# Turning the keys of the late units on VectorE and in SBUF transfers, instead of on TensorE

## The chip, the cores and the metric

The kernel runs on one core of a Trainium2 chip. The metric is the device time of one execution in microseconds; before the change it is 658.83 us, the median of three runs (657.85 to 659.45). The profiled execution has a span of 656.8 us.

## What is computed

The program is a gated linear attention followed by an MLP. All data are float32.

```
f = sigmoid(f_logit)                         # (4, 8, 768, 48): batch, heads, tokens, D
for t in range(768):
    state = f[t][:, None] * state + outer(k[t], v[t])   # a 48 x 48 state per head
    y[t]  = q[t] @ state
x = y as (3072 tokens, 384)                  # heads side by side
h = x @ w_in                                 # (384, 2048)
out = (h * sigmoid(1.702 * h)) @ w_out       # (2048, 384)
```

## The kernel before, in words

The tokens are cut into 12 units of U = 256 tokens (three per batch element), each with all 8 heads as NP = 4 pairs. A tile `X` holds queries and keys of a unit with the head dimension on partitions (two heads of a pair in two halves of 64 rows) and tokens along the free dimension. The recurrence over tokens is not run step by step. Six levels of doubling blocks (1, 2, 4, ... 32 tokens) each give a masked score product: `score` (L384) multiplies queries by keys, `evacuate` (L410) applies the mask, `add` (L448) multiplies by the values, and `promote` (L439) multiplies queries and keys by the block's gates, so that after the last level the keys in `X` carry all the gates up to the end of their chunk of 64 tokens. In units 3 to 11 two levels go in one part (`levels`, kind "V"); three V parts make the six levels. In units 0 to 2 each level has a part of its own (kind "W").

Then comes the state. For the products of keys and values over tokens (L523, in the part of kind "S") the keys have to lie with tokens on partitions: in `t["kn"]`. Before the change two parts of kind "T" do this (`turn_k`, L498 to L506): four transpositions of 128x128 on TensorE (L505) into a PSUM tile `tkn`, and a copy by ScalarE (L506) into `kn`; twice a unit. L523 uses `kn` as the stationary operand and the v rows as the moving one; L538 to L543 on VectorE fold the products into the states; L563 multiplies queries by states, and L571 copies the outputs into `yT`, which goes by transfers within SBUF (L592, L597) into `xT`, the MLP's input.

The MLP is the fill: a list of small steps (h: L727, sigmoid L732, g L733; in the late units the output products L704), which `merge` deals out between the attention parts. It gives each part a share (V 4, S 3, T 1, B 1, W 3), sums them over a unit, and after each part emits fill in proportion. So the number and order of the parts also set how much MLP work stands between any two of them.

TensorE runs its instructions in the order written out by this code. Up to unit 3 so do the other engines; after that a scheduler orders VectorE, ScalarE, GpSimd and the transfer queue. All transfers are issued by SyncE, in order; a transfer also waits for the one eight places ahead of it.

For units 3 to 11 queries, keys and gates come in raw and are turned by VectorE (`turn`, L327), in the parts of kind "B" of the unit before (`begin_f`, `begin`, `begin_k`). Where these parts go is set in `parts_of`: `i - 3` counts back from the end of the list of parts.

Of the kernel before, what the change touches and what calls it, by code (L numbers as in the profile page):

```python
# [9 lines left out]
F32 = mybir.dt.float32  # L10
# [13 lines left out]
def kernel(  # L24
# [33 lines left out]
    nc = tc.nc  # L58
    B, H, S, D = q.shape
    DM = H * D  # L60
    DFF = moe_w_in.shape[1]
    P = 128
    C = 64
    G = 128
    U = 256
    NG = U // G
    NC = U // C
    NU = S // U
    NP = H // 2
    HS = 64  # L70
# [6 lines left out]
    N_FILL = 3  # L77
    N_TURN = 2
    NA = NP * U
# [5 lines left out]
    att = ctx.enter_context(tc.tile_pool(name="att", bufs=1))  # L85
    wp = ctx.enter_context(tc.tile_pool(name="wp", bufs=2))
    mlp = ctx.enter_context(tc.tile_pool(name="mlp", bufs=2))
# [44 lines left out]
    X = const.tile([P, 3, NX], F32, name="X")  # L132
# [17 lines left out]
    for r in range(NGR):  # L150
        ffs = range(r * FG, (r + 1) * FG)
        for ff in ffs[::2]:
            f = slice(ff * P, (ff + 2) * P)
# [122 lines left out]
    def load_vl(n, l):  # L276

        if n >= NALL:
            return
        t = vls[n, l] = ld.tile([P, DM], F32, tag=f"vl{l}", name=f"vl_{n}_{l}")  # L280
        if n < N_TURN:
            pt = ps.tile([P, DM], F32, tag="mm", name=f"tv_{n}_{l}", bufs=4)
            for g in range(NG):
                nc.tensor.matmul(
                    pt[g * 64:(g + 1) * 64], lhsT=perm[:, l - 1, :] if l else ident[:, ::2], rhs=vns[n][:, g, :],
                    start=True, stop=True,
                )
            nc.scalar.copy(t, pt)  # L288
            return
        nc.sync.dma_start(out=t, in_=v_toks[n % 2].rearrange("(n two m) e -> two n m e", two=2, m=LEV[l])[0])  # L290

    def load_vn(n):
        if n >= NALL:
            return
        vns[n] = (mlp if n == 1 else ld).tile([P, NG, DM], F32, tag="osb" if n == 1 else "vn", name=f"vn_{n}", bufs=1)
        if n < N_TURN:
            b, s0 = n // NU, n % NU * U
            for g in range(NG):
                nc.sync.dma_start(
                    out=vns[n][:, g].rearrange("p (h d) -> p h d", h=H),  # L300
                    in_=v[b, :, s0 + g * P:s0 + (g + 1) * P, :].rearrange("h p d -> p h d"),
                )
            return
        nc.sync.dma_start(out=vns[n], in_=v_toks[n % 2].rearrange("(g p) e -> p g e", g=NG))
# [8 lines left out]
    def attention(n):  # L313
# [5 lines left out]
        t = {"tms": [F]}  # L319
        parts = []  # L320

        def part(kind):
            return lambda fn: parts.append((kind, fn))
# [77 lines left out]
        def scores():  # L401
            t["sc"] = ps.tile([P, 2, 512], F32, tag="sc", name=f"sc_{n}_{next(serial)}")
            return t["sc"]
# [65 lines left out]
        def adds(l, c):  # L469
            if l == 0:  # L470
                t["py"] = ps.tile([P, NG, NP, G], F32, tag="y", name=f"y_{n}")
            add(l, slot(t["A"], c), half(LEV[l], 1), start=(l == 0))
            if n + 1 >= N_TURN:
                load_vl(n + 1, l)
# [23 lines left out]
        def turn_k(a0):  # L498
            if a0 == 0:
                t["kn"] = att.tile([P, NP, NG, P], F32, tag="kn", name=f"kn_{n}", bufs=1)  # L500
            pt = ps.tile([P, 2, NG, P], F32, tag="mm", name=f"tkn_{n}_{a0}", bufs=4)
            for a in range(2):
                for g in range(NG):
                    x = (a0 + a) * U + g * G
                    nc.tensor.transpose(pt[:, a, g, :], X[:, 1, x:x + G], ident)  # L505
            nc.scalar.copy(t["kn"][:, a0:a0 + 2], pt)  # L506

        for a0 in (0, 2):
            part("T")(lambda a0=a0: turn_k(a0))

        @part("S")
        def _():
            if n >= N_FILL:
                adds(NL - 2, 0)
            adds(NL - 1, 0 if n < N_FILL else 256)

            pd = scores()
            for a in range(NP):
                for g in range(NG):
                    for h in range(2):  # L520
                        for c in range(2):
                            x = (a * NG + g) * D
                            nc.tensor.matmul(  # L523
                                pd[h * HS:(h + 1) * HS, c, x:x + D],
                                lhsT=t["kn"][c * C:(c + 1) * C, a, g, h * HS:(h + 1) * HS],
                                rhs=vns[n][c * C:(c + 1) * C, g, (2 * a + h) * D:(2 * a + h + 1) * D],
                                start=True, stop=True,
                            )
            if n + 1 >= N_TURN:
                load_vn(n + 1)  # L530
            st = att.tile([P, NC, NP, D], F32, tag="st", name=f"st_{n}", bufs=2)
            D64 = t["tms"][NL].rearrange("p (a c) -> p a c", c=NC)
            prev = t["ahead"] = last.get("st")
            t["before"] = [prev[:, NC - 1] if c == 0 and not first else st[:, c - 1] if c else None for c in range(NC)]
            for c in range(NC):
                d = pd[:, c % 2, :NP * NG * D].rearrange("p (a g e) -> p a g e", a=NP, g=NG)[:, :, c // 2, :]
                if t["before"][c] is None:
                    nc.vector.tensor_copy(st[:, c], d)  # L538
                    continue
                nc.vector.tensor_tensor(  # L540
                    st[:, c], t["before"][c], D64[:, :, c:c + 1].broadcast_to((P, NP, D)), ALU.mult
                )
                nc.vector.tensor_tensor(st[:, c], st[:, c], d, ALU.add)  # L543
            last["st"] = st
# [62 lines left out]
    T = {}  # L607
# [194 lines left out]


    units = [attention(n) for n in range(NALL)]
    LAG = 18 * DM

    def parts_of(n):

        parts = list(units[n][1])
        _, inter = parts.pop()  # L810
        if n:
            kind, scores = parts[0]
            _, ahead = units[n - 1][1][-1]
            parts[0] = kind, lambda: (ahead(), scores())
        if n < N_TURN:

            def with_v(l):
                kind, fn = parts[l]
                return kind, lambda: (fn(), load_vl(n, l) if n == 0 or l else None)
            parts[:NL] = [with_v(l) for l in range(NL)]  # L820
        if n + 1 < NALL:
            begin_f, begin, begin_k, begin_gates = units[n + 1][0]
            i = len(parts)
            if n + 1 < N_FILL:

                parts.append(("K", lambda: (begin_k(), begin_gates(), load_vl(n + 1, 0) if n + 1 < N_TURN else None)))
                parts.insert(i - 4, ("B", begin))
                parts.insert(i - 5, ("B", begin_f))
            else:
                kind, states = parts.pop()  # L830
                parts += [("B", begin_k), (kind, lambda: (states(), begin_gates()))]
                parts.insert(i - 3, ("B", lambda: (begin_f(), begin())))
        else:
            parts.append(("W", inter))
        return parts

    def merge(n, fill, columns, share, pieces=0, hold=0, by=1.0, chores=()):

        parts = parts_of(n)
        total = sum(share(kind) for kind, _ in parts)
        converting = {"W": 3, "T": 3, "B": 1} if n < N_FILL - 1 else {"W": 3, "V": 4, "S": 3, "T": 1, "B": 1}
# [88 lines left out]
```

## Time and profile before

| | |
|---|---|
| time | 658.83 us (657.85 to 659.45) |
| span of the profiled execution | 656.8 us |
| TensorE busy (matmul) | 630.0 us, 96% |
| VectorE busy | 444.7 us, 68% |
| ScalarE busy | 230.2 us, 35% |
| share of the transfer queue's packets in 16 engines' span | 40.4% |
| mean granted TensorE clock | 0.995 |
| transpositions of keys on TensorE (L505) | 96, busy 14.1 us |
| copies of them by ScalarE (L506) | 24, busy 14.0 us |

A group's busy time counts overlapping instructions once; matmuls are pipelined, so the mean length of one (273 ns for L505) is longer than the distance from one to the next. The chain of waits is the better measure of what a group takes on the path. A line of the timeline gives the start, the length, the engine, the line of the code, the operation, and in brackets the idle time before it and what ended that.

### The profile page before, as it was taken

What the parts mean: (1) busy time and instruction counts of PE and PEld (TensorE: products, weight loads), DVE (VectorE), ACT (ScalarE), POOL (GpSimd) and SP (SyncE); (2) the same over time, 40 slices, a digit from 0 to 9 for tenths busy, and PEclk for the clock granted to TensorE, in tenths of its full rate; (3) what the DMA queues carried; (4) which work ended last, traced back from release to release, by engine and by line L of the source; (5) the groups of instructions that cost most, each with busy time, mean ns of one, the idle gap of its engine ahead of it and who ended that gap; (6) DMA issues with size and microseconds to landing.
All of it is one profiled execution on the core that took longest, in us unless ns stands there. A gap on an engine that the chain in (4) does not pass through costs nothing.

```text
span 656.8 us, 20370 instructions
## 1 busy us (share of the span) xinstructions
PE 630.0 (96%) x8946; PEld 541.2 (82%) x8946; DVE 444.7 (68%) x802; ACT 230.2 (35%) x477; POOL 53.4 (8%) x116
## 2 busy tenths in 40 slices
PE   6669999989999999999999999999999999999997
PEld 5546667766678689989989989989989989989997
DVE  2988887788887757657658658558558557553571
ACT  3464443243223423423324324324324324222120
POOL 3020020020001002002002002002002002000000
PEclk9998999999999999999999999999999999999999
DMA  8886975294125444524514515614603202101000
GB/s 190 222 201 164 225 180 133 75 225 78 43 60 151 135 106 117 143 52 118 148 45 121 148 44 120 160 31 119 166 26 104 67 25 62 40 2 26 25 1 24
DMA packets 67554, 67.67 MB, mean 103 GB/s; under 512 B 30410, under 2 KB 61290, under 8 KB 67466
## 3 DMA queue, kind: packets, MB, share of 16 engines
q1 hardware_dynamic: 67466, 66.38, 40.4%
q8 instruction: 70, 1.15, 0.8%
q14 instruction: 18, 0.15, 0.1%
HBM read 56.92 MB, written 8.65 MB: 100 GB/s over the span
## 4 chain that ended last, share of the span: by engine, by line
PE 84%; DVE 9%; ACT 2%; issue 2%; DMA 1%; SPq 0%; DVEq 0%; ACTq 0%
PE h L727 37%; PE o L755 7%; PE o_X L704 7%; PE o_Y L704 7%; PE o_Z L704 7%; PE sc L384 5%; PE y L448 4%; PE o_W L704 4%; PE t L339 2%; PE y L563 2%; PE sc L523 1%; PE tkn L505 1%; DVE X L439 1%; DMA xT<-yT 1%; DVE s L219 1%
## 5 line engine op out<-in xcount | busy, mean ns | idle before, releaser
L727 PE MATMUL h<-xT,w_in 128*128 128x256 f32 (+1 forms) x1152 | 260.4, 382 | 4.7 <-DMA xT<-yT 1.9
L727 PEld LDWEIGHTS h<-xT,w_in 128*128 128x128 f32 x1152 | 215.8, 190 | 38.7 <-issue 3.3
L733 DVE TENSOR_TENSOR g<-h,sg 128x256 f32<-128x256 f32 (+1 forms) x192 | 80.8, 422 | 99.4 <-ACT sg L732 97.0
L732 ACT ACTIVATE sg<-h 128x256 f32<-128x256 f32 (+1 forms) x192 | 73.4, 384 | 192.8 <-PE h L727 186.0
L423 ACT COPY Kc<-X 128x512 f32<-128x512 f32 x69 | 46.1, 668 | 120.4 <-DVE X L439 83.4
L755 PE MATMUL o<-w_out,g 128*128 128x384 f32 x192 | 66.4, 493 | 0.0
L439 DVE TENSOR_TENSOR X<-X,tot 128x1024 f32<-128x1024 f32 x45 | 55.2, 1226 | 15.4 <-PE sc L384 10.2
L755 PEld LDWEIGHTS o<-w_out,g 128*128 128x128 f32 x192 | 35.3, 190 | 22.8 <-issue 1.5
L704 PE MATMUL o_X<-w_out,g 128*128 128x192 f32 x288 | 51.9, 329 | 0.0
L704 PE MATMUL o_Y<-T,S 128*128 128x192 f32 x288 | 51.1, 331 | 0.1
L704 PEld LDWEIGHTS o_Y<-T,S 128*128 128x128 f32 x288 | 46.5, 190 | 2.6 <-DVE u L679 1.3
L704 PEld LDWEIGHTS o_X<-w_out,g 128*128 128x128 f32 x288 | 47.3, 190 | 0.9
L410 DVE TENSOR_TENSOR A<-sc,masks 128x512 f32<-128x512 f32 x72 | 46.7, 679 | 0.0
L448 PE MATMUL y<-A,vl 64*48 64x64 f32 x2304 | 41.3, 218 | 0.1
L448 PEld LDWEIGHTS y<-A,vl 64*48 64x48 f32 x2304 | 36.5, 121 | 3.5 <-issue 3.1
L376 POOL TENSOR_TENSOR tot<-F 128x512 f32<-128x512 f32 x12 | 12.5, 1040 | 327.9 <-DVE st L540 327.9
L327 DVE STREAM_TRANSPOSE X<-raw 128x1024 f32<-128x1024 f32 x18 | 36.7, 2039 | 2.4 <-PE y L563 2.4
L384 PE MATMUL sc<-X,Kc 48*64 48x64 f32 x1344 | 28.6, 222 | 8.5 <-DVE A L410 4.2
L384 PEld LDWEIGHTS sc<-X,Kc 48*64 48x64 f32 x1344 | 24.3, 136 | 15.1 <-ACT vl L288 6.0
L571 ACT COPY yT<-y 48x512 f32<-48x512 f32 x48 | 27.9, 580 | 13.9 <-PE y L563 13.3
L376 POOL TENSOR_TENSOR tot<-tot 128x256 f32<-128x256 f32 (+4 forms) x60 | 26.9, 448 | 4.7
L704 PE MATMUL o_Z<-w_out,g 128*128 128x192 f32 x144 | 26.6, 331 | 0.0
(91 smaller groups left out, 650.8 us busy)
## 6 DMA issues: line engine op xcount, KB each, us to landing
vl<-v_tok SPq DMA_DIRECT2D x60, 192.0 KB, 3.0
bits<-in_moe_w_out_dram SPq DMA_DIRECT2D x8, 768.0 KB, 9.7
bits<-in_moe_w_in_dram SPq DMA_DIRECT2D x8, 576.0 KB, 8.0
v_tok<-in_v_dram SPq DMA_DIRECT2D x10, 384.0 KB, 4.4
vn<-v_tok SPq DMA_DIRECT2D x10, 384.0 KB, 6.8
xT<-yT SPq DMA_DIRECT2D x24, 144.0 KB, 2.9
raw<-in_f_logit_dram SPq DMA_DIRECT2D x18, 192.0 KB, 4.2
raw<-in_q_dram SPq DMA_DIRECT2D x18, 192.0 KB, 3.7
```

Of the source, the lines that this page charges most:

```text
L327: nc.vector.transpose(out.rearrange("p (a i j) -> p a j i", a=NP, j=R), raw[:, j].rearrange("p a (j d) -> p (a j) d", j=R)[:, :, :32],)
L376: nc.gpsimd.tensor_tensor(tn, t2[:, :, 0], t2[:, :, 1], ALU.mult)
L384: nc.tensor.matmul(out[g * HS:(g + 1) * HS, h, a, :], lhsT=lhs(h, a * U + g * G), rhs=rhs(h, a * U + g * G), start=True, stop=True,)
L410: nc.vector.tensor_tensor(A[:, :, c:c + w].rearrange("p h (x t) -> p h x t", t=64), t["sc"][:, :, c:c + w].rearrange("p h (x t) -> p h x t ...
L423: nc.scalar.copy(c.rearrange("p (n m) -> p n m", m=m), X[:, j, :NA].rearrange("p (n two m) -> p n two m", two=2, m=m)[:, :, hf, :],)
L439: nc.vector.tensor_tensor(qk, qk, by, ALU.mult)
L448: nc.tensor.matmul(dst(h, g, a), lhsT=vls[n, u][g * 64:(g + 1) * 64, (2 * a + h) * D:(2 * a + h + 1) * D], rhs=A(h, g, a), start=(start an ...
L704: nc.tensor.matmul(t[bank], lhsT=lhs(f), rhs=rhs(f), start=(new and f == 0), stop=(f == HF - 1), skip_group_check=True,)
L727: nc.tensor.matmul(ph, lhsT=w_in[:, c, ff * P:(ff + 1) * P], rhs=xTs[n][:, c, :], start=(c == 0), stop=(c == NK - 1))
L732: nc.scalar.activation(sg, ph, AF.Sigmoid, scale=1.702)
L733: nc.vector.tensor_tensor(g[ff // FG][:, ff % FG, :], ph, sg, ALU.mult)
L755: nc.tensor.matmul(t["po"], lhsT=g[ff // FG][:, ff % FG, tt * P:(tt + 1) * P], rhs=w_out[:, ff, :], start=(ff == ffs[0]), stop=(ff == ffs[ ...
```

## The change

In units 4 to 11 the keys are brought to token rows without TensorE and PSUM. After the last V part, `carry_k` makes two transpositions of 32x32 blocks on VectorE, one for each half of 128 tokens (`g`), from `X` into a tile `z`. A block transposition leaves each block in its own group of 32 partitions, so 16 transfers for each half move 32 partitions of 512 bytes each (4 pairs x 32 columns) from `z` to the right rows of `kn`: 32 transfers a unit, on SyncE's queue. `kn` has another order of its free dimensions now, and L523 (L543 after) reads it accordingly. The two T parts of these units are gone from the list, and with them their share of fill. The aim is to take these transpositions off TensorE and their copies off ScalarE.

The insertion of the part that turns the next unit's gates and queries, `parts.insert(i - 3, ...)`, becomes `parts.insert(3, ...)`. For the units without T parts that is the same place behind the three V parts; for unit 3 too. In unit 2, which has six level parts and two T parts, it was index 6 and is now index 3.

```diff
-        for a0 in (0, 2):
-            part("T")(lambda a0=a0: turn_k(a0))
+        def carry_k():
+
+            t["kn"] = att.tile([P, NG, P, NP], F32, tag="kn", name=f"kn_{n}", bufs=1)
+            nb = G // 32
+            for g in range(NG):
+                z = mlp.tile([P, nb, 32, NP], F32, tag="sum", name=f"z_{n}_{g}", bufs=3)
+                nc.vector.transpose(
+                    z.rearrange("p b d a -> p a b d"),
+                    X[:, 1, :NA].rearrange("p (a g b t) -> p g a b t", a=NP, g=NG, b=nb)[:, g],
+                )
+                for b in range(nb):
+                    for i in range(P // 32):
+                        nc.sync.dma_start(
+                            out=t["kn"][b * 32:(b + 1) * 32, g, i * 32:(i + 1) * 32, :], in_=z[i * 32:(i + 1) * 32, b]
+                        )
+
+        if n <= N_FILL:
+            for a0 in (0, 2):
+                part("T")(lambda a0=a0: turn_k(a0))
+        else:
+            i_v, (kind, fn) = len(parts) - 1, parts[-1]
+            parts[i_v] = kind, lambda: (fn(), carry_k())
...
-                                lhsT=t["kn"][c * C:(c + 1) * C, a, g, h * HS:(h + 1) * HS],
+                                lhsT=(t["kn"][c * C:(c + 1) * C, a, g, h * HS:(h + 1) * HS] if n <= N_FILL else
+                                      t["kn"][c * C:(c + 1) * C, g, h * HS:(h + 1) * HS, a]),
...
-                parts.insert(i - 3, ("B", lambda: (begin_f(), begin())))
+                parts.insert(3, ("B", lambda: (begin_f(), begin())))
```

## The prediction

> **What bounds the kernel now.** I read the page's engine table first, then the groups by line, then the chain of waits over one late unit, then VectorE's and the transfer queue's order of time over the same stretch, and last TensorE's granted clock.
>
> ```profile
> span 656.8 us, 20370 instructions
> PE 630.0 (96%) x8946; PEld 541.2 (82%) x8946; DVE 444.7 (68%) x802; ACT 230.2 (35%) x477; POOL 53.4 (8%) x116
> ```
>
> TensorE is busy 96% of the span, and its row of 40 slices is 9 almost everywhere after the first tenth: in the late units nothing but TensorE's own stream sets the time. Work taken off it there is worth its full length, and a wait put into its stream, whose order is written out, costs its full length too.
>
> ```profile
> L505 PE MATMUL tkn<-ident,X 128*128 128x128 f32 x96 | 14.1, 273 | 1.1 <-DVE X L436 1.1
> L506 ACT COPY kn<-tkn 128x512 f32<-128x512 f32 x24 | 14.0, 585 | 2.8 <-PE tkn L505 1.9
> L327 DVE STREAM_TRANSPOSE X<-raw 128x1024 f32<-128x1024 f32 x18 | 36.7, 2039 | 2.4 <-PE y L563 2.4
> ```
>
> The first two groups are what is replaced, for 8 of the 12 units; the third is the nearest row for VectorE's transposition. Now the chain through unit 7, from its last scores (L384) to the products that read the turned keys (L523). Columns: start, length, what.
>
> ```profile
> 379.96 0.76 PE sc L384 x52
> 380.72 0.90 PE y L448 x64
> 381.62 10.56 PE h L727 x48
> 392.17 0.44 PE tkn L505 x4
> 392.61 2.59 PE h L727 x12
> 395.20 0.44 PE tkn L505 x4
> 395.64 1.30 PE h L727 x6
> 396.94 1.95 PE o_X L704 x12
> 398.89 1.04 PE y L448 x64
> 399.93 0.92 PE sc L523 x64
> ```
>
> There is no gap in it. Call 380.72, the end of these scores, T0: the turned keys are wanted at T0 + 19.2. VectorE in the same stretch:
>
> ```profile
> 380.79 1.23 DVE L439 TENSOR_TENSOR X<-X,tot 128x1024 f32<-128x1024 f32 x1 [0.28 <-PE sc L384]
> 381.93 1.28 DVE L410 TENSOR_TENSOR A<-sc,masks 128x512 f32<-128x512 f32 x2
> ```
>
> The keys have their last value only when L439 is done, T0 + 1.3; it cannot start before the scores have read the old one. So the whole of the new path, transposition, transfers and landing, has to fit between T0 and the products. Only the transfers that carry attention outputs (yT to xT, L597) go within SBUF here; their issue on SyncE, their time to landing and two of them in a row:
>
> ```profile
> L597 SPq DMA_DIRECT2D xT<-yT x48: 507/587/1557, 48.1 to 602.0; - x48
> DMA to landing us min/median/max: 1.7/2.2/2.5
> 413.11 1.22 SPq L597 DMA_DIRECT2D xT<-yT  x2
> ```
>
> Issuing one takes SyncE 587 ns (median), 0.61 us from start to start (1.22 for two), for only 16 or 32 partitions of 1 KB.
>
> **What the Trainium skill says.** "VectorE: DVE Perf Modes", The three transpose paths: VectorE transposes 32x32 blocks independently, so crossing the blocks of partitions needs something else; that is why 16 transfers follow each transposition. The trace has block transpositions only, and agrees. "DMA: Bandwidth & Descriptors", Issuing engines are not separate DMA queues: the time on the sequencer to start a DMA "is usually small relative to the DMA itself". Here it is not: 0.59 us of 2.2 us. "TensorE: Matmul & The Clock Gate", Part 1: after an idle window of about 3.4 us the clock is halved, and comes back after about as long a busy one. The trace shows one such spell. In these rows the number after the comma behind POOL is the granted clock:
>
> ```profile
> 44.00:48.00 4.00, 1.40 (x64) 1.11 (x64) 2.44 (x5) 2.26 (x4) 3.24 (x5) 0.89 0.80 229
> 48.00:52.00 4.00, 3.21 (x68) 2.07 (x68) 4.00 (x9) 2.36 (x5) 0.22 (x1) 0.50 0.37 89
> 52.00:56.00 4.00, 3.69 (x15) 2.70 (x14) 1.47 (x5) 0.86 (x2) 0.00 (x0) 0.76 0.60 112
> ```
>
> TensorE stood idle 2.68 us until 48.80 after sparse work, ran at 0.50, and was back at full clock only some 5 us later.
>
> **The change, part by part.**
>
> *Removed from TensorE:* two groups of four transpositions in each of units 4 to 11. In the chain each group is 0.44 us, so 2 x 0.44 x 8 = 7.0 us, all of it on the path. ScalarE loses 16 copies x 0.585 = 9.4 us; at 35% busy it was not the bound, so that is worth nothing.
>
> *Added to VectorE:* 16 transpositions of 128x512. L327 takes 2.04 us for 128x1024, so 1.02 each, 16.3 us in all. VectorE is 68% busy. In the built order both stand behind L410, which ends at T0 + 2.5 (383.21), so the first is done at T0 + 3.5; the second hides behind the issue of the first 16 transfers. Behind them in the order stands the turn of the next unit's keys, and then the MLP's g; TensorE may run short of PSUM buffers for about 1 us, but inside the stretch that is followed by the wait below, so it costs nothing more.
>
> *Added to SyncE's queue:* 32 transfers per unit, 32 partitions of 512 B each, all on one queue. The profile has no such transfer, so I bound the issue: from below by the 0.44 us at which loads of raw follow each other (398.05 to 399.36 for four issues, 1.31 / 3), and at the very least the 0.36 us of a store of the output; from above by 0.61 us of the transfers within SBUF. I take 0.61: same pair of memories, no larger partition count, and the issue did not shrink with size there (median 576 ns for L592's 144 KB, 595 ns for the last token's transfers of under 1 KB). From the first issue at T0 + 3.55, the last starts at 3.55 + 31 x 0.61 = T0 + 22.5, and lands 2.2 us later, at T0 + 24.7. The waits of a transfer on one eight places ahead don't bind: 8 x 0.61 is longer than 2.2. Queued behind the 32 are loads of raw keys, the v rows and f_logit for later units; their users come a stretch or more later, so I cost them at nothing. The two v loads ahead of them wait for L448, done at T0 + 0.9, and are issued before the transposition ends.
>
> *Moved:* without the two T parts the fill of MLP work is dealt out anew. Between T0 and the products there stood 66 records of h and 12 of o_X; the built order now has 54 and 6 (for unit 11: 36 of h alone). The h records took (10.56 + 2.59 + 1.30) / 66 = 0.219 us each, o_X 1.95 / 12 = 0.163. So TensorE arrives at the products at T0 + 0.90 + 54 x 0.219 + 6 x 0.163 + 1.04 = T0 + 14.7; in unit 11 at 0.90 + 36 x 0.219 + 1.04 = T0 + 9.8. The change thus wants the keys 4.5 us earlier than before.
>
> *The new wait:* 24.7 - 14.7 = 10.0 us in each of units 4 to 10, 24.7 - 9.8 = 14.9 in unit 11: 7 x 10.0 + 14.9 = 84.9 us. TensorE's whole stream stands behind it. Everything else catches up meanwhile, so nothing comes back later.
>
> *The clock:* each such wait is long enough for the halved clock. The spell above lasted 5.1 us after work resumed (48.80 to about 53.9, as 0.76 over 4 us means half clock for 1.9 us); the skill's window is 3.4 us. Half of 3.4 to 5.1 us is lost, 1.7 to 2.6; I take 2.0, so 16 us for eight.
>
> *Also edited:* the turn of unit 3's gates and queries, inside unit 2, now comes three parts earlier (insertion at index 3, where i - 3 was 6). It moves two 2-us transpositions and eight loads on queues that have some slack there; I cost it at 0, with 2 us either way.
>
> Sum: 658.8 - 7.0 + 84.9 + 16 = 752.7 us; forecast 752.
>
> **Rivals.**
> 1. *The same wait, cheaper issue.* At 0.44 us the last transfer lands at 3.55 + 31 x 0.44 + 2.2 = T0 + 19.4: waits of 4.7 us, and 9.6 in unit 11, 42.5 together, with the clock 16: 658.8 - 7 + 42.5 + 16 = 710. At 0.37 they are 2.5 and 7.4, 25 together, with the clock only partly lost (6): 683. For it: these copies are plain 32x128 blocks. Against: even the tiniest transfers within SBUF took as long as the large ones.
> 2. *Hidden, and faster.* If the queue issued so fast that all landed before T0 + 14.7, that is 0.29 us each, only the 7.0 us would remain: 652. For it: the same number of bytes, 0.5 MB a unit, is little for the engines. Against: no issue in this trace is under 0.31 us.
> 3. *VectorE or landing comes on top.* If g stands ahead of the transpositions, or landing takes 4.2 us as loads of raw do[...]: 8 x 2 us more, 768.
>
> **How the numbers follow.** Forecast 0.62; cheap issue 0.28 (0.20 at 710, 0.08 at 683); hidden 0.04; on top 0.06. The range leaves out the hidden case, the cheapest issue and what lies beyond 768: 692 to 768. Faster by over 0.2%: 0.04; within: 0.01; slower: 0.95.
>
> **What would show it.** L505 at 32 records instead of 96; the new transfers with about 0.6 us each from start to start on SyncE; TensorE's largest wait before the products, on these transfers, near 10 us in each of units 4 to 10 and longer in 11, with eight dips of the clock. It is wrong if the issue is much under 0.5 us, if the transpositions take 2 us each or don't follow L410 at once, or if the clock holds.

## The result, and the profile after

The changed kernel takes 762.6 us (median of four runs, 759.71 to 766.1), against 658.34 us before (median with a fourth run beside the three above): a ratio of 1.1588 (95% interval 1.1533 to 1.1644). It is slower by 104 us; 94 were forecast, and the time lies inside the range.

From the page of the changed kernel, the span, the engines' busy time, and the chain that ended last, by engine and by line:

```profile
span 757.9 us, 20677 instructions
PE 662.9 (87%) x8882; PEld 566.9 (75%) x8882; DVE 459.2 (61%) x818; ACT 217.5 (29%) x461; POOL 55.7 (7%) x116
...
PE 63%; SPq 16%; DVE 10%; issue 5%; DMA 4%; ACT 2%; DVEq 0%; ACTq 0%
PE h L748 23%; SPq L520 15%; PE o_X L725 7%; PE o L776 6%; PE o_Y L725 6%; PE o_Z L725 6%; PE sc L384 4%; PE o_W L725 3%; PE sc L543 2%; DMA kn<-z 2%; PE y L448 2%; DVE z L514 2%; PE y L584 1%; DVE A L410 1%; DVE X L327 1%
```

SPq is the queue on SyncE that issues transfers. It was 0% of the chain before; now the issue of the new transfers (L520) is 15% of the span, some 115 us. L505 is down to 32 records.

The order of time over unit 7, the stretch shown before. The last scores end at 417.43 here, which is T0. First VectorE, then the queue, then TensorE, each from the changed kernel:

```profile
419.84 2.05 DVE L514 STREAM_TRANSPOSE z<-X 128x512 f32<-128x512 f32 x2
421.93 2.03 DVE L327 STREAM_TRANSPOSE X<-raw 128x1024 f32<-128x1024 f32 x1
```

```profile
420.98 20.75 SPq L520 DMA_DIRECT2D kn<-z  x32
```

```profile
424.26 6.74 PE L748 MATMUL h<-xT,w_in 128*128 128x256 f32 x30 [0.56 <-DVE g L754]
430.84 1.14 PE L725 MATMUL o_X<-w_out,g 128*128 128x192 f32 x6
431.91 1.11 PE L448 MATMUL y<-A,vl 64*48 64x64 f32 x64
432.94 1.25 PE L543 MATMUL sc<-vn,kn 64*64 64x48 f32 x8
436.71 0.40 PE L543 MATMUL sc<-vn,kn 64*64 64x48 f32 x2 [2.52 <-DMA kn<-z]
441.77 0.67 PE L543 MATMUL sc<-vn,kn 64*64 64x48 f32 x4 [4.66 <-DMA kn<-z]
443.00 1.88 PE L543 MATMUL sc<-vn,kn 64*64 64x48 f32 x50 [0.55 <-DMA kn<-z]
444.81 3.46 PE L725 MATMUL o_X<-w_out,g 128*128 128x192 f32 x10
```

The first transfer is issued at T0 + 3.55; the 32 issues take 20.75 us, 0.65 us each; TensorE arrives at the products at T0 + 15.5 and goes through them in steps, as the transfers land, until the last 50 records start at 443.00, T0 + 25.6. From arrival to these last records it is 10.06 us; 14 records run in between, and TensorE stands idle for 7.7 us of it. Then even what has its data is slow: ten records of o_X take 3.46 us, where in the kernel before each took 0.163. The granted clock, the share of TensorE's full speed, shows why. A row gives a stretch and its length, the busy time of PE, PEld, DVE, ACT and POOL with their instructions, and after the comma the granted clock, the transfers' share and GB/s:

```profile
433.00:443.00 10.00, 2.27 (x19) 1.86 (x15) 0.34 (x1) 0.00 (x0) 0.00 (x0) 0.74 0.11 26
443.00:445.00 2.00, 2.00 (x51) 1.91 (x52) 0.08 (x1) 0.00 (x0) 0.00 (x0) 0.50 0.98 246
445.00:447.00 2.00, 2.00 (x7) 2.00 (x8) 1.83 (x6) 0.00 (x0) 0.00 (x0) 0.50 0.88 200
447.00:449.00 2.00, 2.00 (x11) 2.00 (x10) 1.14 (x3) 0.32 (x1) 1.55 (x2) 0.74 0.90 185
```

Half clock until about 448, 5 us into the work that follows the wait.

### The profile page after: what moved, and what is told of

Read it like the earlier page. It is cut to its first block, busy times and chain, and to the rows that moved or that the text cites. A ratio compares the mean times of both kernels' runs of the same rounds, so it can differ in the third digit from the quotient of the medians.

```text
span 757.9 us, 20677 instructions
## 1 busy us (share of the span) xinstructions
PE 662.9 (87%) x8882; PEld 566.9 (75%) x8882; DVE 459.2 (61%) x818; ACT 217.5 (29%) x461; POOL 55.7 (7%) x116
## 4 chain that ended last, share of the span: by engine, by line
PE 63%; SPq 16%; DVE 10%; issue 5%; DMA 4%; ACT 2%; DVEq 0%; ACTq 0%
PE h L748 23%; SPq L520 15%; PE o_X L725 7%; PE o L776 6%; PE o_Y L725 6%; PE o_Z L725 6%; PE sc L384 4%; PE o_W L725 3%; PE sc L543 2%; DMA kn<-z 2%; PE y L448 2%; DVE z L514 2%; PE y L584 1%; DVE A L410 1%; DVE X L327 1%
## 5 line engine op out<-in xcount | busy, mean ns | idle before, releaser
L753 ACT ACTIVATE sg<-h 128x256 f32<-128x256 f32 (+1 forms) x192 | 71.6, 382 | 182.6 <-PE h L748 171.2
L754 DVE TENSOR_TENSOR g<-h,sg 128x256 f32<-128x256 f32 (+1 forms) x192 | 78.6, 420 | 68.9 <-ACT sg L753 67.3
L543 PE MATMUL sc<-vn,kn 64*64 64x48 f32 x768 | 38.0, 281 | 70.0 <-DMA kn<-z 68.3
L543 PEld LDWEIGHTS sc<-vn,kn 64*64 64x64 f32 x768 | 33.4, 184 | 73.4 <-issue 46.4
L564 DVE TENSOR_TENSOR st<-st,sc 128x192 f32<-128x192 f32 x44 | 15.6, 354 | 76.3 <-PE sc L543 74.8
L725 PE MATMUL o_X<-w_out,g 128*128 128x192 f32 x288 | 61.6, 371 | 0.0
L725 PEld LDWEIGHTS o_X<-w_out,g 128*128 128x128 f32 x288 | 56.6, 221 | 1.1
L690 ACT COPY p<-o_X 128x192 f32<-128x192 f32 x9 | 2.9, 318 | 120.3 <-PE o_X L725 120.3
```

What stands on the lines that cost most here:

```text
L543: nc.tensor.matmul(pd[h * HS:(h + 1) * HS, c, x:x + D], lhsT=(t["kn"][c * C:(c + 1) * C, a, g, h * HS:(h + 1) * HS] if n <= N_FILL else t[ ...
L725: nc.tensor.matmul(t[bank], lhsT=lhs(f), rhs=rhs(f), start=(new and f == 0), stop=(f == HF - 1), skip_group_check=True,)
L753: nc.scalar.activation(sg, ph, AF.Sigmoid, scale=1.702)
L754: nc.vector.tensor_tensor(g[ff // FG][:, ff % FG, :], ph, sg, ALU.mult)
```

## The experiments

The theory (A): the keys come late because one queue issues 32 transfers one after another, at 0.63 to 0.65 us each. Rivals: bytes, landing or VectorE (B); the MLP work that now stands elsewhere (C). Each ratio is to runs of the kernel before on the same chip; their medians lie between 658.3 and 660.2 us, so a difference of one or two us between two times of the table says nothing.

| run | us | ratio to before, 95% interval |
|---|---|---|
| half the transfers, same bytes | 684.01 | 1.0374, 1.0324 to 1.0425 |
| two queues | 683.31 | 1.0357, 1.0333 to 1.0380 |
| empty T parts back | 739.45 | 1.1209, 1.1181 to 1.1238 |
| through DRAM | 671.67 | 1.0174, 1.0140 to 1.0208 |
| strided order alone, in the kernel before | 667.31 | 1.0131, 1.0099 to 1.0163 |
| TensorE kept at work in the wait | 758.58 | 1.1506, 1.1474 to 1.1539 |
| no transfers | 664.96 | 1.0086, 1.0062 to 1.0111 |
| through DRAM, contiguous, with room | 654.58 | 0.9931, 0.9906 to 0.9956 |
| unit 2's part alone, in the kernel before | 659.71 | 1.0001, 0.9983 to 1.0018 |
| contiguous keys in the changed kernel | 765.37 | 1.1615, 1.1568 to 1.1662 |
| through DRAM, contiguous, without room | 663.31 | 1.0047, 1.0031 to 1.0063 |

### Half the transfers, the same bytes

One tile `z` holds both halves here.

```diff
+            z = att.tile([P, NG, nb, 32, NP], F32, tag="A", name=f"z_{n}", bufs=2)
...
-                        nc.sync.dma_start(
-                            out=t["kn"][b * 32:(b + 1) * 32, g, i * 32:(i + 1) * 32, :], in_=z[i * 32:(i + 1) * 32, b]
...
+                    nc.sync.dma_start(
+                        out=t["kn"][b * 32:(b + 1) * 32, :, i * 32:(i + 1) * 32, :], in_=z[i * 32:(i + 1) * 32, :, b]
```

> The same bytes in half as many transfers: one transfer carries both halves of 128 tokens (32 partitions of 2 x 512 B), 16 a unit instead of 32, after both block transpositions. Theory A (the serial issue of the transfers on SyncE, 0.63 us each, sets the wait): last issue at T0 + 4.7 + 15 x 0.635 = T0 + 14.2, landed at T0 + 16.2 against an arrival of TensorE at T0 + 15.5, so waits of about 1 us and of 6 us in unit 11; 665 to 680 us. Theory B (bytes, landing or VectorE's transpositions set it): no better than 750 us.

78.6 us came back with no byte less: the number of issues sets the wait, and B falls. The 16 issues took 10.25 us in unit 7, 0.64 us each, twice the size and no slower. The time is 4 us above what A allowed; the expectation left out the strided order found below, worth 8 us.

### Two queues

```diff
-                        nc.sync.dma_start(
+                        (nc.gpsimd if i % 2 else nc.sync).dma_start(
```

> Every second of the 32 transfers is issued by GpSimd instead of SyncE. Theory A: SyncE's 16 have landed by T0 + 3.55 + 15 x 0.635 + 1.8 = T0 + 14.9, before TensorE arrives at T0 + 15.5; what remains depends on GpSimd's issue, which no trace shows yet: at 0.63 us each 662 us, at 1 us each a wait of 5 us and about 710 us. Theory B: unchanged, 755 to 765 us.

The time falls as far, by another route: SyncE's 16 issues took 10.06 us in unit 7 and GpSimd's 16, beside them, 7.85. So it is the queue in series, not the transfers, that was slow.

But the time is 21 us above the 662 that the expectation gave for a GpSimd as fast as SyncE, and GpSimd was faster. Some 8 us are the strided order found below. Another part lies in the products, which no marked wait delays in unit 7:

```profile
406.58 3.65 PE L543 MATMUL sc<-vn,kn 64*64 64x48 f32 x64
```

In the run without transfers the same 64 records, with keys in the same order, take 2.08 us. In units 4 to 10 the two-queue run needs 1.4 to 1.6 us more, some 10 us together. Its trace has 16 or 17 semaphore instructions of 51 ns a unit among the weight loads of this line (131 in all); the run without transfers has 3 in all. They are about 0.8 us a unit; what takes the rest is not shown.

### The room of the two T parts back

```diff
             parts[i_v] = kind, lambda: (fn(), carry_k())
+            parts += [("T", lambda: None)] * 2
```

> Two empty T parts stand again in the list of units 4 to 11, so that as much MLP work lies between the last scores and the products as before the change. Theory A: the keys still land at T0 + 25.5, TensorE arrives 3.4 us later (3.9 in unit 11), so 7 x 3.4 + 3.9 = 28 us less: 735 us. If the redistribution of the MLP work were the main cause (theory C), the time would fall to about 655 us.

About 23 us came back, 5 fewer than expected: a wait whose end is fixed from T0 gets shorter by what TensorE arrives later. C as the main cause falls; the lost room is about a fifth of the loss.

### Through DRAM

```diff
+    z_drams = [tc.dram_tile([P, G // 32, 32 * NP], F32, name=f"z_dram{g}") for g in range(NG)]
...
+                nc.sync.dma_start(out=z_drams[g], in_=z.rearrange("p b d a -> p b (d a)"))
+            for g in range(NG):
+                for b in range(nb):
+                    nc.sync.dma_start(
+                        out=t["kn"][b * 32:(b + 1) * 32, g].rearrange("r (i d) a -> r i (d a)", i=P // 32),
+                        in_=z_drams[g].rearrange("(i r) b x -> b r i x", i=P // 32)[b],
+                    )
```

> The transposed blocks go out to DRAM in one transfer for each half of 128 tokens, and come back in four, 10 transfers a unit instead of 32, with twice the bytes and two landings in a row. Theory A: written at about T0 + 6.5, last read issued by T0 + 11, landed by T0 + 14: no wait in units 4 to 10, about 4 us in unit 11; 653 to 662 us. Theory B (bytes or landing): no better than 760 us.

Another way to the same end, with twice the bytes: 91 us below the changed kernel. But 10 us above what A allowed, though unit 7 has no wait for its keys. They themselves are slow (TensorE's order of time, the run through DRAM):

```profile
405.21 2.13 PE L546 MATMUL sc<-vn,kn 64*64 64x48 f32 x64
```

The 64 records took 1.10 us in the kernel before. What differs is the order of kn: the columns of the stationary operand now lie 4 elements apart. The forecast had not costed that.

### The strided order alone

In the kernel before, only the order of kn in units 4 to 11 is that of the changed kernel:

```diff
                 t["kn"] = att.tile([P, NP, NG, P], F32, tag="kn", name=f"kn_{n}", bufs=1)
+                if n > N_FILL:
+                    t["kn"] = t["kn"].rearrange("p a g d -> p (a g d)").rearrange("p (g d a) -> p a g d", a=NP, g=NG)
```

> The kernel before with one part of the change alone: in units 4 to 11 ScalarE's copy writes the turned keys in the order of the changed kernel (head dimension, then pair), so that the 64 columns of each stationary operand of the products lie 4 elements apart. Nothing else differs. If this order is what makes the products take 2.13 us a unit instead of 1.10 where nothing waits (seen in the run through DRAM), they take the same here, and the time is 658 + 8 x 1.0 = 666 us. If the longer products there come from the transfers or the clock, they stay at 1.10 us and the time within 2 us of before.

```profile
402.80 2.08 PE L525 MATMUL sc<-vn,kn 64*64 64x48 f32 x64
```

So the order does it: 0.98 us a unit, 8.4 us in all (667.31 against 658.93; 95% interval 6.5 to 10.7).

### TensorE kept at work in the wait

```diff
             pd = scores()
+            if n > N_FILL:
+                for i in range(N_WARM):
+                    nc.tensor.matmul(
+                        pd[:, i % 2, 384:], lhsT=w_in[:, 0, :P], rhs=w_in[:, 1, :P], start=True, stop=True,
+                    )
```

> The changed kernel with 40 more matmuls (128 columns each, about 0.22 us) in each of units 4 to 11 ahead of the products, into PSUM columns that nothing reads, so that TensorE works on while it would wait; 40 x 0.22 = 8.8 us fit into the wait of 10 us. The transfers and so the end of the wait stay where they are. If the halved clock after the wait costs 2 to 2.5 us a unit, the time falls by 16 to 20 us, to 743 to 747 us; if the clock costs nothing, it stays at 760 to 764 us.

```profile
435.24 9.20 PE L541 MATMUL sc<-w_in 128*128 128x128 f32 x80
444.37 2.60 PE L549 MATMUL sc<-vn,kn 64*64 64x48 f32 x64
446.90 1.89 PE L731 MATMUL o_X<-w_out,g 128*128 128x192 f32 x10
```

Where the clock held, ten records of o_X took 1.89 us instead of 3.46. From the last 50 products to the next use of the states it is 8.79 us in units 5, 8 and 10 of this run, and 10.22 on average over units 4 to 10 of the changed kernel: holding the clock saves 1.4 us a unit here, and would save 11 us in all. The time is only 4 us lower, and the two intervals overlap, so that the time by itself shows no gain. The trace shows two reasons: in units 6, 9 and 11 the clock was halved all the same (0.72, 0.72 and 0.67 over the 6 us that follow), and the 32 issues took 21.26 us on average instead of 20.80, 3.7 us over eight units.

### No transfers

The products read z as VectorE wrote it, and the 256 transfers are gone; the output of these units is not the reference's.

```diff
-                for b in range(nb):
-                    for i in range(P // 32):
-                        nc.sync.dma_start(
-                            out=t["kn"][b * 32:(b + 1) * 32, g, i * 32:(i + 1) * 32, :], in_=z[i * 32:(i + 1) * 32, b]
-                        )
+                t["z", g] = z
...
-                                      t["kn"][c * C:(c + 1) * C, g, h * HS:(h + 1) * HS, a]),
+                                      t["z", g].rearrange("p b d a -> p (b d) a")[c * C:(c + 1) * C, h * HS:(h + 1) * HS, a]),
```

> The changed kernel with its 256 transfers left out: the products of units 4 to 11 read the block-transposed keys as VectorE wrote them, so the output of these units is not the reference's. All else stays: the parts removed, the transpositions on VectorE, the strided order of the stationary operand. Theory A (the wait on the serial issue costs everything, with the clock): 658 - 7 + 8 (stride) + 4.5 (h behind VectorE, 0.56 us a unit) = 664 us. Theory B (VectorE's transpositions or the new distribution of the MLP work cost much by themselves): 700 us or more.

98 us of the 104 hang on the transfers, with the wait and the clock that they bring. And even without any transfers this change would have been slower than the kernel before: what it takes off TensorE, the strided order and the h that waits for VectorE take back.

### Through DRAM, contiguous, with room

Both `kn` and `z` are contiguous in the head dimension here (their lines are left out below).

```diff
...
+                for i in range(ni):
+                    nc.sync.dma_start(
+                        out=z_drams[g][:, :, i],
+                        in_=z[i * 32:(i + 1) * 32].rearrange("r b a d -> r (b a) d"),
+                    )
+            for g in range(NG):
+                for b in range(nb):
+                    nc.sync.dma_start(
+                        out=t["kn"][b * 32:(b + 1) * 32, g].rearrange("r a m -> r (a m)"),
+                        in_=z_drams[g][:, b * NP:(b + 1) * NP].rearrange("r a i d -> r (a i d)"),
+                    )
...
+            parts += [("T", lambda: None)] * 2
```

> The best of what the runs point to: through DRAM with 8 writes and 8 reads a unit (16 issues instead of 32), the keys contiguous as stationary operand again, and the two empty T parts back, so that TensorE comes to the products at about T0 + 18.9. Writes in runs of 128 B land by about T0 + 11, reads by about T0 + 15, so no wait in units 4 to 11; no stride. 658 - 7 + 0 to 4 for VectorE ahead of h: 651 to 655 us, under both kernels. If landing of the small runs takes 5 us more, 660 us.

The queue and TensorE in unit 7 of this run (T0 is 379.15 here):

```profile
382.28 6.65 SPq L520 DMA_DIRECT2D z_dram<-z  x8
389.09 3.74 SPq L526 DMA_DIRECT2D kn<-z_dram  x8
```

```profile
379.97 14.59 PE L756 MATMUL h<-xT,w_in 128*128 128x256 f32 x66
397.38 1.39 PE L551 MATMUL sc<-vn,kn 64*64 64x48 f32 x64
```

The last read is issued before T0 + 13.7, the products start at T0 + 18.2; nothing waits here, and h runs through without a gap. This version beats both kernels: 0.9931 of the time before, some 4.5 of the 7 us that the removal offers. Most of the rest can be seen in the products: they take 1.28 to 1.42 us in units 4 to 10, not the 1.10 of the kernel before. The trace has 39 semaphore instructions of 51 ns among their weight loads, 2.0 us in all, and the kernel before has none there; that they stand for the waits on the transfers is an inference.

### The edit in unit 2 alone

```diff
-                parts.insert(i - 3, ("B", lambda: (begin_f(), begin())))
+                parts.insert(3, ("B", lambda: (begin_f(), begin())))
```

> The kernel before with one part of the change alone: the turn of unit 3's gates and queries is inserted at index 3 of unit 2's parts instead of index 6. The forecast costed it at 0, with 2 us either way: 657 to 661 us. If it were a hidden part of the loss, 664 us or more.

Nothing, within 0.18%: the cost of 0 holds.

### Contiguous keys in the changed kernel

```diff
-            t["kn"] = att.tile([P, NG, P, NP], F32, tag="kn", name=f"kn_{n}", bufs=1)
+            t["kn"] = att.tile([P, NG, NP, P], F32, tag="kn", name=f"kn_{n}", bufs=1)
...
-                z = mlp.tile([P, nb, 32, NP], F32, tag="sum", name=f"z_{n}_{g}", bufs=3)
+                z = mlp.tile([P, nb, NP, 32], F32, tag="sum", name=f"z_{n}_{g}", bufs=3)
...
```

> The changed kernel with its 32 transfers a unit on SyncE's queue, but kn and z in the order pair, then head dimension: the stationary operand is contiguous, VectorE writes runs of 32 elements, and each transfer writes 4 runs of 128 B a partition instead of one of 512 B. The number of issues stays, so the wait stays; the products get back 8 x 1.0 us, and the first transposition ends 0.4 us earlier: 762 - 8 - 3 = 751 us. If the shorter runs make issue or landing slower, above 762 us.

A miss: no gain at all (1.1615 against the changed kernel's 1.1588, intervals overlapping). The last 50 products of unit 7 in this run:

```profile
447.62 1.70 PE L543 MATMUL sc<-vn,kn 64*64 64x48 f32 x50 [0.49 <-DMA kn<-z]
```

1.70 us, against 1.88 with the stride. They run at half clock either way, and there the stride costs 0.2 us, not 1.0: the two losses don't add. Over the whole stretch from these records to the next use of the states nothing is left of it: 10.29 us on average over units 4 to 10, against 10.22 with the stride. What the earlier transposition gave went into the queue: 32 issues took 21.2 us on average instead of 20.8, and the last 50 products start as late as in the changed kernel, at T0 + 25.7 on average in both.

### Through DRAM, contiguous, without room

> The best kernel (through DRAM, contiguous keys) without the two empty T parts, so that TensorE arrives at the products at T0 + 15 (T0 + 9.8 in unit 11) instead of T0 + 19. In the best kernel the last read was issued at T0 + 13.5, so landed at about T0 + 15.5: no or hardly any wait in units 4 to 10, about 5 us in unit 11, and h behind VectorE again by 0 to 0.5 us a unit: 658 to 664 us. If the empty parts are worth nothing, 654 us.

The edit is that of the run with room, without its last line. The room of the two empty parts is worth 1.2% of the time here (1.0047 against 0.9931), and the gain is gone. The trace shows part of the reason: unit 11, which has the least work ahead of its products, waits 3.5 us for the keys, and the clock is halved there (0.50 from 584.1 to 590.1). In units 4 to 10 no wait is marked between the last scores and the products, not for h either. The traced execution took 659.32 us, and the median is 663.31; where the other 4 us go is not shown.

## Why the prediction was right

*What bounds the kernel, and the removal.* TensorE's stream did set the time, and a wait in it cost its length. The 7.0 us for the removed transpositions were not measured by themselves, but fit: no transfers gave 664.96, and 659 - 7 + 8.4 for the stride + 7 x 0.57 for the h that waits for VectorE in units 4 to 10 is 664.4.

*VectorE.* The first issue at T0 + 3.55 is the forecast to the hundredth; the transposition took 1.10 us where 1.02 was taken. In units 4 to 10 h did wait for VectorE's g, 0.56 us a unit, inside the stretch that ends in the wait, as forecast, so it cost nothing more here. Mostly for that TensorE came to the products at T0 + 15.4 on average, not T0 + 14.7; with contiguous keys, where the transposition takes 0.69 us and h does not wait, it came at T0 + 14.7.

*The issue, the choice that mattered.* 0.61 us was taken, from transfers within SBUF; the new ones took 0.589 us each (median), 0.65 from start to start with an occasional long one; they landed in 1.8 us where 2.2 was taken. The last wait ended at T0 + 25.6 in unit 7, 25.7 on average, instead of 24.7. Measured from the forecast's arrival at T0 + 14.7, and less the 14 records that ran during it, that is 10.4 us a unit and 15 in unit 11, 88 us in place of 84.9. The rival with cheaper issue is out by the same number; so is the hidden one. Theory A rests on four runs: half the issues, two queues, DRAM, none.

*The clock.* Each wait did halve it, as forecast. The Trainium skill, "TensorE: Matmul & The Clock Gate", Part 1, gives about 3.4 us of sustained work until it comes back. Here the mean granted clock over the 6 us from the start of the last 50 products lies between 0.55 and 0.69 in the eight units, so half clock lasted 3.7 to 5.4 us of it. Half of that is lost, 18 us over the eight units by this estimate, where 16 was taken. What holding the clock would win depends on the operand: 11 us with the stride in place. With contiguous keys, which are what the forecast reckoned with, the stretch after the wait takes 10.29 us, against 7.7 for the same records at the pace of the kernel before: about 21 us.

*What was not costed.* The strided stationary operand: the changed order of kn was known, but the forecast gave it no price. At full clock it is 8.4 us. In the changed kernel it hides under the half clock, so that the two together are 2.5 us a unit (10.22 us from the last 50 products on, against those 7.7), 20 us. The sum by these terms is -7 + 88 + 20 = 101 of 104; the two traced executions differ by 101 too, and what is left is no more than the spread of the runs.

That the total came within 10 us thus rests on a wait that was 3 us too small and a clock term about 4 us too small, both with the right mechanism, and on luck in one place: the stride that the forecast had overlooked cost the changed kernel no time that the runs can tell from the clock's. For the versions without the wait, the stride and the room decided whether they beat the kernel before.

## What to carry to other kernels

Price a transfer by its issue as well as by its bytes: a block shuffle in many small pieces on one queue took the number of pieces times 0.65 us here, and fewer, larger or rerouted pieces, even through DRAM, can be faster. Each awaited piece seems to cost its reader a little as well. When a step moves to another engine, check the layout that its reader gets, and keep the work that covered its latency in place: removing a part from a list that deals out filler removed cover too. Losses that lie on top of each other, like a stride under a halved clock, show only when the larger one is gone.

## What was not expected of the hardware

- A float32 stationary operand whose columns lie 4 elements apart: a weight load of 64x64 takes 211 ns instead of 135 (medians, L543 after and L523 before), and 64 records of products 2.08 us instead of 1.10.
- VectorE's block transposition of 128x512 took 1.10 us writing elements 16 B apart, and 0.69 us writing runs of 32.
- An issue within SBUF took SyncE 0.59 or 0.60 us (medians) whether it moved 16 or 32 KB; GpSimd's issues of the same transfers took 0.50 us.
- Eight reads from DRAM of 64 KB each were issued in 3.74 us, 0.47 each. With the eight writes before them it was 10.55 us, against 20.75 for 32 small moves within SBUF.
- Semaphore instructions of 51 ns stand among the weight loads of products that read what many transfers wrote: 131 in the run with two queues, where 64 records took 3.65 us in unit 7 and 2.08 without transfers, and 39 in the run through DRAM with room.
